# Linear attention, RMS norm and a SiLU feed-forward layer on one core: wider moves of w_out in every second tile, and shifted places for seven of its blocks

## The chip, the core and the metric

The kernel runs on one core of a Trainium2 chip. Its time is what the device takes for one execution, in microseconds (us); a time is the median of several runs. The profile is of one execution of its own. Its span goes from the first to the last instruction that it recorded.

## What is computed

Cut to what matters, the reference is this:

```python
# q, k, v: (8, 8, 576, 64) float32; w_in: (512, 2048), w_out: (2048, 512) float32
kv  = np.einsum('bhsd,bhse->bhde', k, v)
out = np.einsum('bhsd,bhde->bhse', q, kv)
rms = np.sqrt(np.mean(out * out, axis=-1, keepdims=True) + 1e-06)
x   = (out / rms * g_norm).transpose(0, 2, 1, 3).reshape(4608, 512)
h   = x @ w_in
g   = h * (1.0 / (1.0 + np.exp(-h)))
y   = g @ w_out          # (4608, 512) float32
```

The two products with `w_in` and `w_out` over 4608 tokens are nearly all of the work. This change concerns the second one.

## The kernel before

**Tiles.** The 4608 tokens are nine tiles `t` = 0 to 8 of TN = 512 tokens. The 2048 hidden columns are 16 blocks `f` of 128. Each number of the large products is held as an upper and a lower part in the type float32r, and a product is three matmuls: upper by lower, lower by upper, upper by upper.

**The first product.** In tiles 0 and 1 `products` makes a block of h from four pieces of x, twelve matmul pairs of 128x256 a block. From tile 2 on `pair_step` works on two blocks at a time (`i + 8` and `i`), with seven smaller products in the place of eight (lines 636 and 648): 42 matmuls of 128x256 in a step, eight steps in a tile.

**The second product.** `gate`, or `upper_part` and `lower_part`, make the activated block as `gh` (upper) and `gl` (lower), 128 x 512 each, in three buffers of the pool `gp`. `project` (line 521) multiplies it by one block `wo{f}` of `w_out`: for each of four groups `n` of 128 tokens it loads 128 columns of `gh` or `gl` into TensorE (the stationary operand; PEld in the profile), and moves 512 columns of `wo{f}` through it, into one PSUM bank `acc` of 512 columns. This is done for (gh, lower part of wo), (gh, upper part) and (gl, upper part). Each of the three goes through `halves` (line 483), which cuts the 512 columns into two matmuls of 256; each of the two comes with a load of the same stationary columns. So a block and a group take six matmuls of 128x256. In the last tile the fourth group has two banks of 256 columns, `acc` and `at`.

**The order.** The instructions run in the order in which the code is written. From tile 2 on a step's 42 matmuls are followed by `project` of the two blocks made one step before (`due`), eight groups of six matmuls, with the attention's own matmuls (lines 266 and 301 to 303) between them.

**Places in SBUF.** Where a tile begins in each partition follows from the order and the sizes of the pools. `gap` (line 80) is a tile that nothing uses; it moves those after it. A block of `wo` or `wi` has 2 x 512 x 4 = 4096 bytes, which is 16 x 256, so that in the kernel before all of `wo0` to `wo15` begin at the same place modulo 256, at 192. `x`, `x_second` and `operand`, which are moved in the first product, begin at 192 too; `wi`, `gh` and `gl`, whose columns are the stationary operand, begin at 0. The pieces begin at whole multiples of 512 bytes behind that.

**The scale.** `rsqrt` (line 442) works out the inverse root of the attention's sums by Newton steps on DVE. From batch 2 on it has two tiles of scratch of 72 columns, `m` and `u`.

Of the kernel before, what the change touches and what calls it, by code (L numbers as in the profile page):

```python
# [8 lines left out]
F32 = mybir.dt.float32  # L9
# [21 lines left out]
def linear_attention_rms_silu_ffn(  # L31
# [23 lines left out]
    B, NP, P, S = q.shape  # L55
    D = P // 2
    DM = NP * P
    NF = w_in.shape[0]
# [7 lines left out]
    weights = ctx.enter_context(tc.tile_pool(name="weights", bufs=1))  # L66
# [3 lines left out]
    small = ctx.enter_context(tc.tile_pool(name="small", bufs=2))  # L70
    gp = ctx.enter_context(tc.tile_pool(name="gp", bufs=LAG + 1))
# [5 lines left out]

    def gap(pool, size, name):  # L80
        pool.tile([P, size // 4], F32, name=name, bufs=1)

    def weights_places():
        for kind in ("wo", "wi"):
            for f in range(NF):
                block(kind, f, F32)
            if kind == "wo":
                gap(weights, 64, "gap_weights")

    gap(const, 128, "gap_first")  # L90
    gap(kvq, 192, "gap_q")
    gap(gp, 64, "gap_gated")
    kvm = [const.tile([P, P], F32, name=f"kvm{i}") for i in range(NP)]
    for t in kvm:
        nc.gpsimd.memset(t, 0.0)
# [4 lines left out]
    for i in range(4):  # L100
        nc.gpsimd.tensor_copy(
            out=both[32 * i:32 * i + 32, 32 * (i ^ 1):32 * (i ^ 1) + 32], in_=ident[32 * i:32 * i + 32, 32 * i:32 * i + 32]
# [36 lines left out]
    def block(kind, f, dtype):  # L139
        return weights.tile([P, 2, NP * P], dtype, name=f"{kind}{f}", tag=f"{kind}{f}")  # L140

    weights_places()

    def load_block(kind, f):
# [89 lines left out]
    def newton(y, u, m, eps=0.0):  # L234

        return [
            lambda: nc.vector.scalar_tensor_tensor(out=u, in0=m, scalar=eps, in1=y, op0=ALU.add, op1=ALU.mult),
            lambda: nc.vector.scalar_tensor_tensor(out=u, in0=u, scalar=-0.5, in1=y, op0=ALU.mult, op1=ALU.mult),
            lambda: nc.vector.scalar_tensor_tensor(out=y, in0=u, scalar=1.5, in1=y, op0=ALU.add, op1=ALU.mult),
        ]  # L240
# [201 lines left out]
    def rsqrt(sums, y, on_tensor):  # L442

        n = NP * (S // 32)
        sums, y = (t.rearrange("p c j -> p (c j)") for t in (sums, y))
        if on_tensor:
            bank = at_bank()
            m, u = bank[:, 0:n], bank[:, n:2 * n]
            nc.tensor.matmul(out=m, lhsT=both, rhs=sums, start=True, stop=True)
            calls = [lambda: nc.vector.tensor_scalar(  # L450
                out=m, in0=m, scalar1=float(D) * EPS, scalar2=None, op0=ALU.add
            )]
        else:
            m, u = (small.tile([P, n], F32, name=name, bufs=1) for name in ("m", "u"))
            calls = [
                lambda i=i: nc.vector.tensor_copy(
                    out=m[32 * i:32 * i + 32], in_=sums[32 * (i ^ 1):32 * (i ^ 1) + 32]
                )
                for i in range(4)
            ]  # L460
            calls.append(lambda: nc.vector.scalar_tensor_tensor(
                out=m, in0=m, scalar=float(D) * EPS, in1=sums, op0=ALU.add, op1=ALU.add
            ))
        calls.append(lambda: nc.vector.tensor_scalar(
            out=y.bitcast(I32), in0=m.bitcast(I32), scalar1=-0.5, scalar2=RSQRT_MAGIC, op0=ALU.mult, op1=ALU.add
        ))
        return calls + 3 * newton(y, u, m)
# [10 lines left out]
    def at_bank(tag=None):  # L478

        at_tags.append(at_tags.pop(0))  # L480
        return ps_at.tile([P, 512], F32, name="at", tag=tag or at_tags[-1])

    def halves(to, stationary, moving, start, stop):


        n = to.shape[-1]
        for at in range(0, n, 256):
            nc.tensor.matmul(  # L488
                out=to[:, at:at + 256], lhsT=stationary, rhs=moving[:, at:at + 256],
                start=start and at == 0, stop=stop and at == n - 256,  # L490
            )

    def products(hp, t, f, c):
        w = parts["wi", f]
        fs = slice(c * P, (c + 1) * P)
        for i, (a, b) in enumerate(((0, 1), (1, 0), (0, 0))):
            halves(
                hp[:, :TN], w[:, a, fs], x_part(t, b, c), c == 0 and i == 0, c == NP - 1 and i == 2
            )
# [12 lines left out]
    def sums_of(t):  # L512

        whole, half = slice(0, DM), (slice(0, DM // 2), slice(DM // 2, DM))
        banks = [(acc_bank(), n, whole) for n in range(TN // P)]
        if t == NT - 1:
            last, n, _ = banks.pop()
            banks += [(last, n, half[0]), (at_bank(), n, half[1])]
        return banks

    def project(t, f, gh, gl, bank, n, cs):
        first, last = order(t)[0], order(t)[-1]
        w = parts["wo", f]
        ns = slice(n * P, (n + 1) * P)
        bank = bank[:, :cs.stop - cs.start]
        for i, (g, a) in enumerate(((gh, 1), (gh, 0), (gl, 0))):
            halves(bank, g[:, ns], w[:, a, cs], f == first and i == 0, f == last and i == 2)
        if f == last:
            ob = tmp.tile([P, S], F32, name="ob", tag="tmp")[:, :cs.stop - cs.start]
            (nc.scalar.copy if n % 2 else nc.vector.tensor_copy)(out=ob, in_=bank)  # L530
            nc.sync.dma_start(out=out[t * TN + n * P:t * TN + (n + 1) * P, cs], in_=ob)
# [9 lines left out]
    def order(t):  # L541

        if t < 2:
            return [(f + t * HF) % NF for f in range(NF)]
        return [f for i in range(HF) for f in (i + HF, i)]
# [43 lines left out]
    def load_sums(i, *halves):  # L589

        for half in halves:
            to = place(f"sums{half}", half, F32R)
            nc.sync.dma_start(
                out=to.rearrange("p a j n -> p (a j n)").bitcast(F32),
                in_=sums_in_dram[i % HF, half].rearrange("p a n -> p (a n)"),
            )
# [72 lines left out]
    def pair_step(t, i, groups):  # L669
# [5 lines left out]
        def due(n):  # L675
            while n > 0 and groups:
                n -= (groups[0][-1].stop - groups[0][-1].start) / DM
                project(*groups.pop(0))
# [80 lines left out]
    def plan(b, g):  # L759
# [48 lines left out]
        if b == 1:  # L808
            at(chains, s, lambda: rsqrt(*norms, True))
        else:  # L810
            spread_out(lambda: rsqrt(*norms, False), 3 * s + 2, 6, 3, 3, 3)
# [11 lines left out]
    with tc.manual_schedule():  # L823

        first = [FirstPair(c) for c in range(NP)]
        stats = at_bank().rearrange("p (c i j) -> p c i j", i=2, j=8)
        second = plan(1, 3)
        for item in ORDER.split():
            kind, n = item.rstrip("0123456789"), int(item.lstrip("wiopbg") or 0)
# [150 lines left out]
        for t in range(NT):  # L980
            sums = sums_of(t)
# [6 lines left out]
            for step, f in enumerate(order(t)):  # L988
                g = t * NF + step
                for job in first_jobs.pop(g, ()):  # L990
                    job()
                for item in prepped:
                    split_block(*item, nc.scalar.copy)
                prepped = []
                if t == 0:
                    prepped = [("wi", f + 2)] * (3 <= f + 2 < NF) + [("wo", f)] * (f > 0)
                run(sum((bits(*item) for item in prepped), []), *[call() for call in chains.pop(g, ())])
                if t == 0 and 3 < f + 3 < NF:
                    magnitude("wi", f + 3)
                if t == 0 and f < WARM:  # L1000
                    hp = warm[f]
                    products(hp, t, f, NP - 1)
                else:
                    hp = h_bank()
                    for c in range(NP):
                        products(hp, t, f, c)
                pend.append(((t, f, *gate(t, hp)), sums))
                if t == 0 and f + 1 < NF:
                    magnitude("wo", f + 1)
                for job in mid_jobs.pop(g, ()):  # L1010
                    job()
                if len(pend) > LAG:
                    item, olds = pend.pop(0)
                    for old in olds:
                        project(*item, *old)
                for job in last_jobs.pop(g, ()):
                    job()
# [4 lines left out]
        for old in sums:  # L1022
            for item, _ in pend:
                project(*item, *old)
# [41 lines left out]
```

## Time and profile before

| | |
|---|---|
| median of 3 runs | 827.99 us (827.68 to 828.14) |
| the profiled execution | 827.72 us, its span 825.9 us |
| PE busy | 815.1 us (99%), 7518 instructions |
| PEld busy (loads of the stationary operand) | 808.5 us (98%), 7518 |
| DVE busy | 527.6 us (64%), 1027 |
| ACT busy | 358.4 us (43%), 744 |
| POOL busy | 145.6 us (18%), 142 |
| DMA | 122.81 MB, 149 GB/s over the span |

PE is TensorE's matmuls and PEld its weight loads, which overlap them. A matmul's end is modelled in the profile and lies behind the start of the next one, so the busy time of one matmul (276 ns) is not what it costs: that is the distance from its start to the next one's. A timeline row holds the start of its first instruction, the time to the end of its last, and after "x" how many it merges; the start of the next row minus its own start is what these took.

### The profile page before, as it was taken

How to read it: one execution, taken by the hardware profiler on the slowest of the kernel's cores; microseconds unless marked ns; L12 is line 12 of the kernel's file. 1: busy time of each engine (PE TensorE's matmuls, PEld its weight loads, DVE VectorE, ACT ScalarE, POOL GpSimd, SP SyncE). 2: the span in 40 equal slices, each digit the busy share in tenths (PEclk: the TensorE clock that was granted, in tenths of full speed). 3: DMA queues.
4: the chain of work that ended last, by engine and by line, in shares of the span. 5: the costliest groups of instructions: out<-in, count | busy, mean ns of one | idle time of the engine just before them, and what ended most of it. 6: DMA issues, size and time to landing. Idle time of an engine off the chain costs nothing.

```text
span 825.9 us, 18181 instructions
## 1 busy us (share of the span) xinstructions
PE 815.1 (99%) x7518; PEld 808.5 (98%) x7518; DVE 527.6 (64%) x1027; ACT 358.4 (43%) x744; POOL 145.6 (18%) x142
## 2 busy tenths in 40 slices
PE   8989999999999999999999999999999999999998
PEld 7889999999999999999999999999999999999998
DVE  4886884888476567757676668656765764464332
ACT  4766554534363255325442455225533423243222
POOL 2786883423020002000200011001100000000000
PEclk9999999999999999999999999999999999999999
DMA  8879011246352635364424453454423343334331
GB/s 324 321 245 380 7 42 70 102 182 233 126 177 95 218 120 169 103 214 149 168 77 163 161 182 103 143 177 160 143 92 104 108 159 106 106 106 155 103 103 52
DMA packets 42434, 122.81 MB, mean 149 GB/s; under 512 B 4848, under 2 KB 5104, under 8 KB 42352
## 3 DMA queue, kind: packets, MB, share of 16 engines
q1 hardware_dynamic: 42352, 121.65, 42.2%
q8 instruction: 59, 0.97, 0.5%
q14 instruction: 23, 0.19, 0.1%
HBM read 103.81 MB, written 17.83 MB: 147 GB/s over the span
## 4 chain that ended last, share of the span: by engine, by line
PE 94%; DMA 4%; POOL 1%; ACT 0%; issue 0%; SPq 0%
PE acc L488 46%; PE hp L654 32%; PE hp L488 9%; PE at L266 2%; DMA wo<-in_moe_w_out 1%; DMA k<-in_k 1%; DMA v<-in_v 1%; PE at L302 1%; PE at L303 1%; PE at L301 1%; DMA wi<-in_moe_w_in 1%; PE at L488 1%; DMA early_wi<-in_v 1%; PE at L299 1%; POOL wo L204 0%
## 5 line engine op out<-in xcount | busy, mean ns | idle before, releaser
L488 PE MATMUL acc<-wo,gh 128*128 128x256 f32 x2272 | 353.6, 277 | 0.0
L488 PEld LDWEIGHTS acc<-wo,gh 128*128 128x128 f32 x2272 | 302.1, 188 | 1.0 <-POOL wo L204 0.2
L488 PE MATMUL acc<-wo,gl 128*128 128x256 f32 x1136 | 222.9, 276 | 0.5 <-POOL gl L507 0.5
L488 PEld LDWEIGHTS acc<-wo,gl 128*128 128x128 f32 x1136 | 171.8, 188 | 0.7 <-POOL gl L507 0.7
L654 PE MATMUL hp<-x_second,wi 128*128 128x256 f32 x1344 | 163.1, 276 | 0.0
L654 PEld LDWEIGHTS hp<-x_second,wi 128*128 128x128 f32 x1344 | 157.2, 188 | 0.0
L654 PE MATMUL hp<-operand,wi 128*128 128x256 f32 x1008 | 123.3, 276 | 0.0
L654 PEld LDWEIGHTS hp<-operand,wi 128*128 128x128 f32 x1008 | 118.4, 188 | 0.0
L288 POOL TENSOR_TENSOR ql<-q,qh 128x576 fp32r<-128x576 f32 x24 | 35.3, 1472 | 368.2 <-ACT qh L287 321.7
L705 ACT COPY wi<-hp 128x256 f32<-128x256 f32 x56 | 20.8, 372 | 136.8 <-PE hp L654 136.8
L663 ACT ACTIVATE gh<-gf 128x512 fp32r<-128x512 f32 x56 | 35.4, 633 | 91.9 <-DVE gf L718 80.3
L663 ACT ACTIVATE gh<-wi 128x512 fp32r<-128x512 f32 x56 | 35.5, 634 | 76.6 <-DVE wi L718 66.3
L706 DVE TENSOR_TENSOR gf<-hp,wi 128x256 f32<-128x256 f32 x28 | 11.9, 425 | 81.6 <-ACT wi L705 81.6
L706 DVE TENSOR_TENSOR wi<-hp,wi 128x256 f32<-128x256 f32 x28 | 11.9, 425 | 81.2 <-ACT wi L705 81.2
L488 PE MATMUL hp<-x,wi 128*128 128x256 f32 x360 | 46.4, 283 | 1.4 <-POOL wi L204 1.4
L488 PE MATMUL hp<-x_second,wi 128*128 128x256 f32 x384 | 46.3, 276 | 0.0
L488 PEld LDWEIGHTS hp<-x,wi 128*128 128x128 f32 x360 | 43.5, 189 | 2.2 <-POOL wi L204 1.6
L667 DVE TENSOR_TENSOR gl<-wi,gh 128x512 fp32r<-128x512 f32 x56 | 38.4, 685 | 11.3 <-ACT wi L664 11.3
L488 PEld LDWEIGHTS hp<-x_second,wi 128*128 128x128 f32 x384 | 44.9, 188 | 0.1
L667 DVE TENSOR_TENSOR gl<-gf,gh 128x512 fp32r<-128x512 f32 x56 | 39.2, 700 | 7.4 <-ACT gf L664 7.4
L707 DVE TENSOR_TENSOR wi<-hp,wi 128x256 f32<-128x256 f32 x56 | 23.8, 425 | 29.5 <-PE hp L654 29.5
L307 ACT ACTIVATE sq<-at 128x256 f32<-128x256 f32 (+1 forms) x56 | 22.9, 410 | 44.5 <-PE at L303 35.7
(142 smaller groups left out, 1011.1 us busy)
## 6 DMA issues: line engine op xcount, KB each, us to landing
wi<-sums_in_dram SPq DMA_DIRECT2D x112, 512.0 KB, 3.3
out<-ob SPq DMA_DIRECT2D x35, 256.0 KB, 2.4
wi<-in_moe_w_in SPq DMA_DIRECT2D x16, 512.0 KB, 7.9
wo<-in_moe_w_out SPq DMA_DIRECT2D x16, 512.0 KB, 8.7
sums_in_dram<-sum_parts SPq DMA_DIRECT2D x16, 512.0 KB, 3.0
k<-in_k SPq DMA_DIRECT2D x28, 288.0 KB, 5.1
v<-in_v SPq DMA_DIRECT2D x28, 288.0 KB, 5.2
q<-in_q SPq DMA_DIRECT2D x28, 288.0 KB, 3.7
```

The source lines that it names most:

```text
L266: nc.tensor.matmul(out=self.kv[h], lhsT=self.k[rows, c, :], rhs=self.v[rows, c, :], start=(start and r == 0), stop=(stop and r == 4),)
L288: nc.gpsimd.tensor_tensor(out=self.ql, in0=self.q, in1=self.qh.bitcast(F32), op=ALU.subtract)
L299: nc.tensor.matmul(out=ps, lhsT=self.kvm, rhs=self.q[:, w], start=True, stop=True)
L301: nc.tensor.matmul(out=ps, lhsT=self.kh, rhs=self.ql[:, w], start=True, stop=False)
L307: nc.scalar.activation(out=self.sq[:, self.w], in_=self.ps, func=AF.Square)
L488: nc.tensor.matmul(out=to[:, at:at + 256], lhsT=stationary, rhs=moving[:, at:at + 256], start=start and at == 0, stop=stop and at == n - 256,)
L654: nc.tensor.matmul(out=out, lhsT=a_of(i, a, c), rhs=x[:, b, c], start=(n == 0), stop=(n == 5))
L663: nc.scalar.activation(out=gh, in_=x, func=AF.Silu)
L667: nc.vector.tensor_tensor(out=gl, in0=x, in1=gh.bitcast(F32), op=ALU.subtract)
L705: nc.scalar.copy(out=p1, in_=u)
L706: nc.vector.tensor_tensor(out=c1[:, low], in0=v, in1=p1, op=ALU.add)
L707: nc.vector.tensor_tensor(out=u2, in0=y, in1=p1, op=ALU.add)
```

## The change

In tiles 2, 4, 6 and 8 `project` has `halves` move 512 columns in one matmul; in tiles 0, 1, 3, 5 and 7 it moves 256 as before. The two banks of 256 columns of the last tile stay as they are. A gap of 32 bytes is put ahead of each of `wo9` to `wo15`, so that `wo9` begins at 224 modulo 256, and the next ones at 0, 32, 64, 96, 128 and 160; `wo0` to `wo8` stay at 192. The gap behind the `wo` blocks and that in `gp` grow, and `u` in `rsqrt` takes the place of the sums that it no longer needs (288 bytes less), so that every other tile stays where it was modulo 256.

```diff
     def weights_places():
         for kind in ("wo", "wi"):
             for f in range(NF):
+                if kind == "wo" and f > NF // 2:
+                    gap(weights, 32, f"gap{f}")
                 block(kind, f, F32)
             if kind == "wo":
-                gap(weights, 64, "gap_weights")
+                gap(weights, 96, "gap_weights")
...
-    gap(gp, 64, "gap_gated")
+    gap(gp, 96, "gap_gated")
...
-            m, u = (small.tile([P, n], F32, name=name, bufs=1) for name in ("m", "u"))
+            m, u = small.tile([P, n], F32, name="m", bufs=1), sums
...
-    def halves(to, stationary, moving, start, stop):
+    def halves(to, stationary, moving, start, stop, piece=256):
         n = to.shape[-1]
-        for at in range(0, n, 256):
+        piece = min(n, piece)
+        for at in range(0, n, piece):
             nc.tensor.matmul(
-                out=to[:, at:at + 256], lhsT=stationary, rhs=moving[:, at:at + 256],
-                start=start and at == 0, stop=stop and at == n - 256,
+                out=to[:, at:at + piece], lhsT=stationary, rhs=moving[:, at:at + piece],
+                start=start and at == 0, stop=stop and at == n - piece,
             )
...
-            halves(bank, g[:, ns], w[:, a, cs], f == first and i == 0, f == last and i == 2)
+            halves(
+                bank, g[:, ns], w[:, a, cs], f == first and i == 0, f == last and i == 2,
+                DM if t and t % 2 == 0 else DM // 2,
+            )
```

Two places show it in the order of TensorE's instructions; lines 488 and 492 are the matmul in `halves`, 301 to 303 (304 to 306 after) the attention's product for a later batch. The number behind a tile's name tells buffers apart, and "x4" is four equal instructions in a row. The first place is the first step of tile 2, before:

```order
L654 MATMUL hp_3255<-x_second_115,wi11_2919 128x256 x6
L301 MATMUL at_3323<-ql_3167,kh_3192 128x320
L302 MATMUL at_3323<-qh_3166,kl_3193 128x320
L303 MATMUL at_3323<-qh_3166,kh_3192 128x320
L488 MATMUL acc_3105<-wo8_1227,gh_3198 128x256 x4
L488 MATMUL acc_3105<-wo8_1227,gl_3200 128x256 x2
L488 MATMUL acc_3106<-wo8_1227,gh_3198 128x256 x4
L488 MATMUL acc_3106<-wo8_1227,gl_3200 128x256 x2
```

The same place on TensorE in the changed kernel:

```order
L661 MATMUL hp_3261<-x_second_115,wi11_2925 128x256 x6
L304 MATMUL at_3329<-ql_3173,kh_3198 128x320
L305 MATMUL at_3329<-qh_3172,kl_3199 128x320
L306 MATMUL at_3329<-qh_3172,kh_3198 128x320
L492 MATMUL acc_3111<-wo8_1234,gh_3204 128x512 x2
L492 MATMUL acc_3111<-wo8_1234,gl_3206 128x512
L492 MATMUL acc_3112<-wo8_1234,gh_3204 128x512 x2
L492 MATMUL acc_3112<-wo8_1234,gl_3206 128x512
```

Six matmuls of 256 columns have become three of 512; nothing has changed its place. This happens to 240 such groups of six. The second place is the end of tile 8 on TensorE in the changed kernel, where the third group is moved at 512 columns and the fourth, with its two banks, still at 256:

```order
L492 MATMUL acc_9104<-wo7_1149,gh_9841 128x512 x2
L492 MATMUL acc_9104<-wo7_1149,gl_9843 128x512
L492 MATMUL acc_9105<-wo15_1831,gh_9840 128x256 x2
L492 MATMUL acc_9105<-wo15_1831,gl_9842 128x256
L492 MATMUL acc_9105<-wo7_1149,gh_9841 128x256 x2
L492 MATMUL acc_9105<-wo7_1149,gl_9843 128x256
L492 MATMUL at_9106<-wo15_1831,gh_9840 128x256 x2
```

Here, too, only the width has moved. On ACT, POOL and the DMA queue the order and the shapes are the same in both kernels; on DVE 54 instructions of the Newton steps write or read `sums` where they had `u`.

## The prediction

> **What bounds the kernel now.** I read the page's busy times and clock first, then who waited for whom on TensorE, then the timeline of its matmuls.
>
> ```profile
> span 825.9 us, 18181 instructions
> PE 815.1 (99%) x7518; PEld 808.5 (98%) x7518; DVE 527.6 (64%) x1027; ACT 358.4 (43%) x744; POOL 145.6 (18%) x142
> PEclk9999999999999999999999999999999999999999
> PE 94%; DMA 4%; POOL 1%; ACT 0%; issue 0%; SPq 0%
> ```
>
> TensorE is busy for 99% of the span at the full granted clock, and it is 94% of the chain that ended last. The waits of PE (total, times, longest) are these, first and last row of seven:
>
> ```profile
> PE hp L844 <- POOL ident masks.py:199: 1.9, 1, 1.9
> ...
> PE acc L488 <- POOL gl L507: 0.5, 1, 0.5
> ```
>
> All seven together are 7.6 us. In the middle of the span there is no idle time at all (busy time of PE, PEld, DVE, ACT, POOL, then clock and DMA share):
>
> ```profile
> 300.00:400.00 100.00, 100.00 (x956) 99.60 (x951) 65.00 (x135) 43.43 (x97) 7.44 (x5) 1.00 0.45 150
> ```
>
> So the time is the sum over TensorE's matmuls of the distance from one start to the next, and the change is worth what it does to these distances. The timeline of a step in tile 3 gives the usual one:
>
> ```profile
> 270.36 0.62 PE L488 MATMUL acc<-wo,gh 128*128 128x256 f32 x4
> ...
> 273.08 2.20 PE L654 MATMUL hp<-operand,wi 128*128 128x256 f32 x18
> 275.12 2.09 PE L654 MATMUL hp<-x_second,wi 128*128 128x256 f32 x17
> ```
>
> From 270.36 to 273.08 lie four groups of six, 24 matmuls in 2.72 us, **113.3 ns** each; then 18 in 2.04 us, again 113.3. It isn't the only value that matmuls of this shape and these places take. In tile 0, with no clock loss and no transfer under way (the second fence, a row by stretches):
>
> ```profile
> 86.30 0.64 PE L488 MATMUL acc<-wo,gh 128*128 128x256 f32 x4
> ...
> 89.13 1.10 PE L488 MATMUL hp<-x,wi 128*128 128x256 f32 x8
> ```
>
> ```profile
> 86.30:89.10 2.80, 2.80 (x26) 2.80 (x25) 2.59 (x5) 2.60 (x6) 1.93 (x3) 1.00 0.00 0
> ```
>
> 24 matmuls take 2.83 us, **117.9 ns** each. PE is fully busy there and waits for nobody: the matmul and the load of the next stationary columns, which run beside each other, fit together less well. So 4.5 ns of a matmul hang on how these two reads meet, and the change alters that in two ways.
>
> **The change part by part.** What it touches is here:
>
> ```profile
> L488 PE MATMUL acc<-wo,gh 128*128 128x256 f32 x2272 | 353.6, 277 | 0.0
> L488 PE MATMUL acc<-wo,gl 128*128 128x256 f32 x1136 | 222.9, 276 | 0.5 <-POOL gl L507 0.5
> ```
>
> The two rows hold 3408 matmuls, and the last tile's bank `at` has 48 more: 3456 = 9 tiles x 16 blocks x 4 groups x 6.
>
> *The width.* Tiles 2, 4 and 6 have 64 groups of a block each, tile 8 has 48 of full width: 240 groups, and 720 pairs of matmuls that become one each. A pair now costs 2 x 113.3 = 226.7 ns. The trace has no float32r matmul of 512 columns. The nearest row is that of 320 columns, with the same 128x128 load beside it:
>
> ```profile
> 584.61 0.30 PE L301 MATMUL at<-ql,kh 128*128 128x320 f32 x1
> 584.75 0.31 PE L302 MATMUL at<-qh,kl 128*128 128x320 f32 x1
> 584.89 0.31 PE L303 MATMUL at<-qh,kh 128*128 128x320 f32 x1
> 585.04 0.63 PE L488 MATMUL acc<-wo,gh 128*128 128x256 f32 x4
> 585.50 0.39 PE L488 MATMUL acc<-wo,gl 128*128 128x256 f32 x2
> 585.73 0.62 PE L488 MATMUL acc<-wo,gh 128*128 128x256 f32 x4
> ```
>
> From 584.61 to 585.73 are three of 320 columns and six of 256: 1.12 us less 0.68 leaves 0.44, 147 ns each. That is 0.458 ns a column against 0.443 at 256: the longer move is no cheaper by the column, although it has fewer loads. At that rate 512 columns take 235 ns, 8 more than the pair: 720 x 8 = +5.8 us. The other end is a matmul that lasts about as long as one of 512 columns would and has one load of 128 columns under it, the plain float32 one of 256 columns (each is two records, which pass at a lower rate):
>
> ```profile
> 57.08 0.59 PE L299 MATMUL at<-q,kvm 128*128 128x256 f32 x2
> 57.32 0.82 PE L488 MATMUL acc<-wo,gh 128*128 128x256 f32 x4
> 57.98 0.40 PE L488 MATMUL acc<-wo,gl 128*128 128x256 f32 x2
> ```
>
> The 0.90 us hold two such passes and four of 256 columns at 113 to 118 ns (0.45 to 0.47): 215 to 225 ns a pass. At 215 a pair would save 11.7 ns, 720 x 11.7 = -8.4 us. A saving of 6.7 ns, if only the second half of the pair's two extra costs went, would be -4.8 us. I take the middle of 215 and 235, 225 ns: 720 x -1.7 = **-1.2 us**, ends -8.4 and +5.8.
>
> By the Trainium skill ("TensorE: Matmul & The Clock Gate", section "Back-to-back issue gap") a warm matmul of N columns takes N / 2.4 + 2.5 ns: about 109 ns at 256 and 216 at 512. The trace differs at 256, with 113.3. By the page alone a pair would fall from 226.7 to 216, some 7.7 us in all.
>
> *The change of width.* After the three of 320 columns six matmuls of 256 take 0.69 us (585.04 to 585.73) in the place of 0.68: about 10 ns to fall back into step. The widths change in 32 steps (8 in each of four tiles): **+0.3 us**, ends 0 and 1.
>
> *The places.* Seven blocks of `wo` now begin elsewhere relative to the stationary columns: by 32 bytes in `wo9` and in `wo15` (the other way round the 256), up to 128 in `wo12`. Matmuls of 256 columns on them: 7 blocks x 24 in each of tiles 0, 1, 3, 5 and 7, that is 840, and 7 x 6 in the last tile's fourth group: 882. No float32r row of the trace has other places than these, so the price is bounded: nothing, if places don't matter; 4.5 ns, if they bring the state at 86.30; twice that, +7.9 us, if the worst place is as far again from the better state. A gain can't be excluded (a place better than today's), and I bound it by the mirror of the 4.5 ns, -4.0 us. I take 4.5 ns, the one other value that steady matmuls of this shape show: 882 x 4.5 = **+4.0 us**. What the places do to the 315 pairs of 512 columns on these blocks is within the ends of the width's term.
>
> *The rest.* The scratch `u` becomes `sums`: 54 DVE instructions of the same shapes, hidden by TensorE (DVE is busy 65 of 100 us); without this cover they would still take as long as before. The loads of `wo9` to `wo15` land at other places, and none of PE's seven waits names them. The fewer matmuls come sooner by 1% of a tile at the most, which ACT and DVE, at 43% and 65%, follow.
>
> The sum is -1.2 + 0.3 + 4.0 = +3.1 us. Against the profiled execution, 827.72 us, that is 830.8; the median of the runs shown is 0.27 above it, so **831.1 us**.
>
> By the Trainium skill ("SBUF — State Buffer", section "Who interferes with whom") TensorE's two read ports, for the moving operand and for the weights, are independent. Then the places would cost nothing and the sum would be -0.9 us. The two distances, 113.3 and 117.9, for one shape at the same clock don't prove the opposite, but ask for something else that sets them.
>
> **The rivals.**
>
> *The long move hides its load and the places are free.* A load lasts about one 256-column matmul, so behind the first half of 512 nothing runs beside the move. For it speaks the 215 ns of the plain float32 pass, and that matmuls on 64 columns show no effect of the places:
>
> ```profile
> L266 PE MATMUL hp<-early_wo,early_wi 128*64 128x64 f32 x32 | 1.4, 228 | 1.0 <-DMA early_wo<-in_v 1.0
> L266 PE MATMUL hp<-early_wi,early_wo 128*64 128x64 f32 x32 | 1.4, 228 | 0.0
> ```
>
> Their operands begin at 192 and 0 and the other way round, with the same duration. Against it speaks the row of 320 columns. It gives 827.99 - 4.8 to -8.4: 819.6 to 823.2 us with free places, up to 826.3 where these take back a part. The page's 216 ns falls into this case.
>
> *The two cancel, or neither does anything.* 512 columns cost the two of 256 and the places little, or -4 stands against +4: within 1.65 us, 826.3 to 829.6.
>
> *The step is lost and stays lost.* At 86.30 the slower state holds over whole blocks, through both products, though only one meeting of load and move can have begun it. If a change of width or of place throws TensorE into it, the first product's matmuls, which the diff doesn't touch, pay too: 42 in each of 32 steps, 1344 x 4.5 = 6.0 us in the even tiles alone, 837 us with the forecast's sum; in all of tiles 1 to 8 about 5,900 x 4.5 = 26 us, 854 us. Against it: at 585.50 the six matmuls are back at 0.23 us a pair right behind the change of width. It decides as soon as steps behind a 512-column group show 118 ns.
>
> **How the numbers follow.** Forecast (the places cost more than the width saves): 36%, 829.6 to 834. Long move pays: 29%. Cancel: 22%. Step lost: 13%, 834 and more. What this kernel's measurement can tell from no change is about 0.2%, 1.65 us. So faster 29%, same 22%, slower 49%. The range leaves out the lower part of the second case (about 12%) and the upper part of the last (about 8%): 822.8 to 838.
>
> **What would show it.** A group of a block in tile 2 on `wo0` to `wo8` should take three times 225 ns, 0.675 us against 0.68: 0.65 says that the load is hidden, 0.70 that the rate of the 320 columns holds. In tile 3 a group on `wo9` to `wo15` should take 0.707 us, on the others 0.68. The 18 matmuls of a first product behind 512-column groups should take 2.04 us; 2.12 would be the lost step. The forecast is wrong if places cost nothing (0.68 in tile 3), or if the 512 columns take 220 or less.

## The result and the profile after

The changed kernel takes **841.09 us** (median of 4 runs, 840.82 to 841.19) against 828.07 before: a ratio of 1.0157 (95% interval 1.014 to 1.0175), +13.0 us. The forecast was 831.1, with a range of 822.8 to 838: the sign was right, the size four times too small, and the time lies above the range.

These lines of the page after answer to those shown of before: span, busy time by engine, granted clock, and the second product's groups, now in two widths (busy us, mean ns).

```profile
span 839.0 us, 16741 instructions
PE 829.0 (99%) x6798; PEld 790.0 (94%) x6798; DVE 530.6 (63%) x1027; ACT 358.8 (43%) x744; POOL 144.9 (17%) x142
PEclk9999999999999999999999999999999999999999
...
L492 PE MATMUL acc<-wo,gh 128*128 128x256 f32 x1312 | 209.0, 280 | 0.0
...
L492 PE MATMUL acc<-wo,gh 128*128 128x512 f32 x480 | 150.6, 395 | 0.0
L492 PE MATMUL acc<-wo,gl 128*128 128x256 f32 x656 | 131.2, 279 | 0.5 <-POOL gl L511 0.5
...
L492 PE MATMUL acc<-wo,gl 128*128 128x512 f32 x240 | 94.7, 394 | 0.0
```

TensorE has 720 matmuls and 720 loads less, PEld is busy 18.5 us less (790.0 for 808.5), the clock is full, PE is busy for 99% of the span as before and waits for nobody new. All of the 13 us are in the distances between matmuls. For 256 columns I call a distance of 113.3 ns the better step and 117.8 ns the slower one. The timeline shows three kinds of place. Tile 2, the 512-column group on `wo7` (at 192), and the first product behind it:

```profile
317.17 0.62 PE L492 MATMUL acc<-wo,gh 128*128 128x512 f32 x2
...
319.96 2.28 PE L661 MATMUL hp<-operand,wi 128*128 128x256 f32 x18
322.08 0.87 PE L661 MATMUL hp<-x_second,wi 128*128 128x256 f32 x6
```

From 317.17 to 319.96 lie twelve wide matmuls, 2.79 us: **232.5 ns** each, where two of 256 took 226.7. And from 319.96 to 322.08 the first product, which the diff doesn't touch, takes 2.12 us for 18: **117.8** in the place of 113.3, the slower step, as in the prediction's row at 86.30. In tile 3, first product and then `wo12` (at 64), 256 columns:

```profile
367.24 2.88 PE L661 MATMUL hp<-x_second,wi 128*128 128x256 f32 x24
369.96 0.63 PE L492 MATMUL acc<-wo,gh 128*128 128x256 f32 x4
...
372.79 0.40 PE L492 MATMUL acc<-wo,gh 128*128 128x256 f32 x2
```

The first product is at 113.3 here (2.72 us for 24), the 24 on the shifted block take 2.83: 117.9.

I added up the distances from each matmul's start to the next one's over both traces, by kind, and took the difference:

| kind of matmul | before, us | after, us | difference |
|---|---|---|---|
| wide in the changed kernel (720 pairs) | 163.6 | 167.7 | **+4.1** |
| 256 columns on shifted blocks (882) | 100.8 | 104.7 | **+3.9** |
| first product (untouched) | 358.6 | 362.0 | **+3.4** |
| 256 columns on `wo0` to `wo8` (untouched) | 132.5 | 134.2 | **+1.7** |
| attention at lines 301 to 303 | 18.6 | 19.0 | +0.3 |
| all others | 46.5 | 46.3 | -0.2 |
| sum | | | +13.1 |

So 8 us lie in what the diff changes, and 5.4 in matmuls that it doesn't.

### The profile page after: what moved, and what is told of

It reads as the page before. It is cut to its first block, busy times and chain, and to the rows that moved or that the text cites. A ratio compares the mean times of both kernels' runs of the same rounds, so it can differ in the third digit from the quotient of the medians.

```text
span 839.0 us, 16741 instructions
## 1 busy us (share of the span) xinstructions
PE 829.0 (99%) x6798; PEld 790.0 (94%) x6798; DVE 530.6 (63%) x1027; ACT 358.8 (43%) x744; POOL 144.9 (17%) x142
## 4 chain that ended last, share of the span: by engine, by line
PE 96%; POOL 1%; ACT 1%; DMA 1%; issue 1%; SPq 0%; DVE 0%; POOLq 0%
PE acc L492 47%; PE hp L661 32%; PE hp L492 10%; PE at L269 2%; PE at L304 1%; PE at L305 1%; PE at L306 1%; DMA early_wo<-in_v 1%; PE at L492 1%; PE hp L851 1%; PE at L302 1%; PE hp L269 0%; PE acc L357 0%; POOL wo L207 0%; PE acc L370 0%
## 5 line engine op out<-in xcount | busy, mean ns | idle before, releaser
L492 PE MATMUL acc<-wo,gh 128*128 128x256 f32 (+1 forms) x1792 | 359.6, 311 | 0.0
L492 PEld LDWEIGHTS acc<-wo,gh 128*128 128x128 f32 x1792 | 265.4, 188 | 19.3 <-POOL wo L207 0.2
L492 PE MATMUL acc<-wo,gl 128*128 128x256 f32 (+1 forms) x896 | 225.8, 310 | 0.5 <-POOL gl L511 0.5
L661 PE MATMUL hp<-x_second,wi 128*128 128x256 f32 x1344 | 164.6, 277 | 0.0
L661 PEld LDWEIGHTS hp<-x_second,wi 128*128 128x128 f32 x1344 | 158.7, 188 | 0.0
L492 PEld LDWEIGHTS acc<-wo,gl 128*128 128x128 f32 x896 | 145.6, 188 | 11.5 <-POOL gl L511 0.7
L661 PEld LDWEIGHTS hp<-operand,wi 128*128 128x128 f32 x1008 | 121.4, 188 | 2.2
L291 POOL TENSOR_TENSOR ql<-q,qh 128x576 fp32r<-128x576 f32 x24 | 34.7, 1444 | 376.8 <-ACT qh L290 362.0
L492 PE MATMUL hp<-x_second,wi 128*128 128x256 f32 x384 | 47.1, 279 | 0.0
L492 PEld LDWEIGHTS hp<-x_second,wi 128*128 128x128 f32 x384 | 45.7, 188 | 0.1
```

What stands on the lines that cost most here:

```text
L291: nc.gpsimd.tensor_tensor(out=self.ql, in0=self.q, in1=self.qh.bitcast(F32), op=ALU.subtract)
L492: nc.tensor.matmul(out=to[:, at:at + piece], lhsT=stationary, rhs=moving[:, at:at + piece], start=start and at == 0, stop=stop and at == n ...
L661: nc.tensor.matmul(out=out, lhsT=a_of(i, a, c), rhs=x[:, b, c], start=(n == 0), stop=(n == 5))
```

## Experiments

Each is told against the kernel before, run on the same chip beside it. Two theories were open at first: that the width, or that the places, begin the slower step in the untouched matmuls.

### The width alone

The change without its gaps; `u` stays, and the gaps behind `wo` and in `gp` are as before:

```diff
-                if kind == "wo" and f > NF // 2:
-                    gap(weights, 32, f"gap{f}")
...
```

> Only the width: 512 columns in tiles 2, 4, 6 and 8, every block of wo at 192 as in the kernel before. Theory of the width: a 512-column matmul costs 233 ns on wo0 to wo8 in the changed kernel, 6.3 more than two of 256, and would do so on all blocks: 720 x 6.3 = +4.5 us; and if the width is also what throws the first product into the 118 ns step, another 3 to 5 us, +8 to +9.5 in all (836 to 837.5). Theory of the places: the 233 ns come from the shifted blocks ahead of them, and without these a 512-column matmul takes 220 to 226.7: 0 to -4.8 us (823 to 828), with the first product at 113.3 everywhere.

Measured: 832.73 us against 828.0, ratio 1.0059 (1.0044 to 1.0074), +4.7. Twelve wide matmuls of tile 6:

```profile
644.67 0.63 PE L489 MATMUL acc<-wo,gh 128*128 128x512 f32 x2
...
647.47 0.73 PE L658 MATMUL hp<-operand,wi 128*128 128x256 f32 x5
```

2.80 us, 233.3 ns each; by kind the wide ones are +4.4 us, the first product +0.2 and the narrow second one +0.2. The wide move has a price of its own, 6 to 7 ns over the pair that it replaces, and behind the wide blocks of tiles 2, 4 and 6 the first product is in the better step.

### The places alone

The change without its width:

```diff
-                DM if t and t % 2 == 0 else DM // 2,
+                DM // 2,
```

> Only the places: wo9 to wo15 shifted, 256 columns everywhere. Matmuls of 256 columns on the seven blocks are now 7 x 24 x 9 = 1512. If the changed kernel's 118.6 ns hold for them: 1512 x 5.3 = +8.0 us, 836 us. Theory of the places for the lost step: the first product also shows steps at 118 ns behind them, +10 to +13 us (838 to 841). Theory of the width for the lost step: the first product is at 113.3 everywhere and the time is 836 at most. If the places cost nothing by themselves: 828.

Measured: 838.83 us, ratio 1.0132 (1.0115 to 1.0149), +10.8. By kind: shifted blocks +6.9 us, first product +1.8, narrow ones on `wo0` to `wo8` +2.0. So the places alone begin the slower step. The two parts don't simply add up (+4.7 and +10.8 for +13.0): where the 720 pairs lie, the width alone costs 4.4 us, the places alone 4.0, and both together 4.1. In tile 7 (the blocks come in the order of the program, `wo14` begins at 738.94 and `wo6` at 741.78):

```profile
738.94 0.64 PE L492 MATMUL acc<-wo,gh 128*128 128x256 f32 x4
...
741.78 0.64 PE L492 MATMUL acc<-wo,gh 128*128 128x256 f32 x4
...
744.61 2.28 PE L661 MATMUL hp<-operand,wi 128*128 128x256 f32 x18
746.73 2.99 PE L661 MATMUL hp<-x_second,wi 128*128 128x256 f32 x24
749.56 0.64 PE L492 MATMUL acc<-wo,gh 128*128 128x256 f32 x4
```

`wo14` takes 118.3 ns, `wo6`, which has its old place, 117.9, and the first product behind it 117.8 (2.12 us for 18, 2.83 for 24). In this run's trace as a whole the mean distances at 224, 0, 32, 64, 96, 128 and 160 are 118.2, 119.2, 116.8, 117.8, 119.5, 118.6 and 117.7 ns (without breaks of over 200 ns): none of the seven places is as good as 192.

### All blocks at one other place

The kernel before with the gap ahead of the `wo` blocks in the place of behind them:

```diff
+            if kind == "wo":
+                gap(weights, 64, "gap_weights")
             for f in range(NF):
                 block(kind, f, F32)
-            if kind == "wo":
-                gap(weights, 64, "gap_weights")
```

> All 16 blocks of wo begin at 0 modulo 256 in the place of 192; 256 columns everywhere, all else where it was. If a block's place relative to the stationary columns sets the distance, each of the 3456 matmuls takes what wo10 took in the changed kernel, 119.5 ns: 3456 x 6.2 = +21 us, 849 us. If it is the change from one block's place to the next's that costs, and a place held by all is free: 828 to 830 us. If wo10's 119.5 were the lost step and not the place: 113 to 118 mixed, 828 to 844.

Measured: 849.11 us, ratio 1.0255 (1.024 to 1.0271), +21.1, of which the second product is 19.7 by kind. One block of tile 6, and the start of the first product behind it:

```profile
698.60 0.64 PE L488 MATMUL acc<-wo,gh 128*128 128x256 f32 x4
...
701.48 2.22 PE L654 MATMUL hp<-operand,wi 128*128 128x256 f32 x18
```

24 matmuls in 2.88 us, 120.0 ns. The place itself has the price, not the change from one place to the next.

### Which operand's place?

Three runs move one operand, the other, or all. In these, and in the runs with four blocks and with one block further down, `u` is `sums`, as in the change, and the gap in `gp` makes up for it. First both `wo` (to 0, by the edit above) and `gh`, `gl` (to 64):

```diff
-    gap(gp, 64, "gap_gated")
+    gap(gp, 160, "gap_gated")
```

> As the run with all blocks of wo at 0, and gh and gl moved from 0 to 64 with them, so that the distance between moved and stationary operand is what it was before (192 behind). Theory of the relative place: 113.3 ns, 828 us within 2. Theory of the moved operand's own place: as the run with wo alone at 0 (849 if that holds).

Measured: 843.78 us, ratio 1.0191 (1.0176 to 1.0206), +15.8: neither. The steady 120.0 of `wo` at 0 is gone, and the second product shows 113.3 and 117.8 almost alone, mostly the latter, and the first product, which wasn't touched, +3.6 us. In tile 7 the two products change the step from one to the other:

```profile
694.40 0.64 PE L488 MATMUL acc<-wo,gh 128*128 128x256 f32 x4
...
697.23 2.22 PE L654 MATMUL hp<-operand,wi 128*128 128x256 f32 x18
699.29 2.88 PE L654 MATMUL hp<-x_second,wi 128*128 128x256 f32 x24
702.01 0.63 PE L488 MATMUL acc<-wo,gh 128*128 128x256 f32 x4
```

24 of the second product take 2.83 us, 24 of the first 2.72. So the relative place of the two operands decides between which two steps a product moves. That the products now lie apart by 64 bytes and so put each other out of step is a guess at this point. If it is right, moving everything must cost nothing:

```diff
-    gap(const, 128, "gap_first")
+    gap(const, 192, "gap_first")
...
-    gap(gp, 64, "gap_gated")
+    gap(gp, 96, "gap_gated")
...
```

> The kernel before with every tile of SBUF behind the first gap moved by 64 bytes: wo, x, x_second and operand begin at 0, wi, gh and gl at 64. If only the distance between the moved and the stationary operand counts, and its being the same in both products keeps the better step: 828 us within 1.7, 113.3 ns. If the moved operand's own place counts (wo at 0 gave 849): 840 and more.

Measured: 827.93 us against 828.04, ratio 0.9997 (0.9988 to 1.0007): no change. With `wo` at 0, the place that cost 21 us above:

```profile
702.64 0.62 PE L488 MATMUL acc<-wo,gh 128*128 128x256 f32 x4
...
705.36 2.20 PE L654 MATMUL hp<-operand,wi 128*128 128x256 f32 x18
707.40 0.84 PE L654 MATMUL hp<-x_second,wi 128*128 128x256 f32 x6
```

24 in 2.72 us, 18 in 2.04: 113.3. `wo`, `gh` and `gl` lie here at the same places modulo 256 as in the run before; what differs is the first product's operands and the smaller tiles. So the places of one product do set the step of the other, though no run shows how. As `u` is `sums` here too, that part of the change costs nothing. And with the loads moved alone, `wo` staying at 192:

```diff
-    gap(gp, 64, "gap_gated")
+    gap(gp, 160, "gap_gated")
```

> Only the stationary operand of the second product moves: gh and gl begin at 64, wo stays at 192, so the moved one lies 128 ahead of it, as wo14 did. Theory of the distance between the two: the price of wo14, 118.6 ns and more with the lost step, 3456 x 5.3 = +18 us, 846 us. Theory that only the moved operand's place counts: 828 us.

Measured: 845.47 us, ratio 1.021 (1.0194 to 1.0225), +17.4. The moved operand is where it was in the kernel before, and its matmuls slow down all the same:

```profile
706.31 0.64 PE L488 MATMUL acc<-wo,gh 128*128 128x256 f32 x4
...
709.16 0.52 PE L654 MATMUL hp<-operand,wi 128*128 128x256 f32 x3
```

24 in 2.85 us, 118.8, the price of `wo14`, which has the same distance. Within a product, what counts is the place of the moved operand **relative to the columns that are loaded**.

### Where the slower step begins, and how long it holds

Only `wo10` to `wo13` shifted, and then only `wo14`:

```diff
             for f in range(NF):
+                if kind == "wo" and f in {10: 64, 11: 32, 12: 32, 13: 32, 14: 96}:
+                    gap(weights, {10: 64, 11: 32, 12: 32, 13: 32, 14: 96}[f], f"gap{f}")
                 block(kind, f, F32)
```

```diff
             for f in range(NF):
+                if kind == "wo" and f in {14: 192, 15: 64}:
+                    gap(weights, {14: 192, 15: 64}[f], f"gap{f}")
                 block(kind, f, F32)
```

> Of the seven shifted blocks only wo10 to wo13 (0, 32, 64, 96); wo9, wo14 and wo15 stay at 192; 256 columns everywhere. In the run with the places alone the matmuls behind these four come back to 113.3 within a few, and those behind wo14 don't. Theory that the lost step is begun by wo14 and wo15: only the blocks' own price is left, 216 x (5.9 + 3.5 + 4.5 + 6.2) = +4.3 us, and some 0.7 for falling back, 833 us; the first product at 113.3 outside tile 0. Theory that any shifted block begins it by chance: four sevenths of +10.8, 834 us, with steps of the first product at 118.

> Only wo14 is shifted, to 128; all else at 192, 256 columns everywhere. Its own price is 216 x 5.3 = +1.1 us. Theory that it begins the lost step, which then holds until something else disturbs it: more than that, from +3 us (a few steps in each tile) to +15 (most of each tile), 831 to 843, with the first product at 118 behind wo14. Theory that each block pays for itself alone: 829.2 us.

Measured: four blocks 834.05 us, ratio 1.0072 (1.0057 to 1.0087), +6.0; one block **834.21** us, ratio 1.0074 (1.0057 to 1.0091), +6.2. With four blocks the own price is 4.0 us, and the rest lies in the other matmuls: the slower step does begin once in the first product, behind `wo11` in tile 1 (at 162.21 us), and ends with the attention's break at 213 us; from tile 2 on it doesn't. So no block is safe, and my sorting of them was half wrong. With one block the own price is 1.1 us, and 5.2 lie elsewhere. Its timeline in tile 6, from the first product ahead of `wo14` (651.30) to the one two blocks on, and then the same in tile 7:

```profile
648.58 2.88 PE L656 MATMUL hp<-x_second,wi 128*128 128x256 f32 x24
651.30 0.64 PE L490 MATMUL acc<-wo,gh 128*128 128x256 f32 x4
...
659.10 2.99 PE L656 MATMUL hp<-x_second,wi 128*128 128x256 f32 x24
661.92 0.28 PE L490 MATMUL acc<-wo,gh 128*128 128x256 f32 x1
```

```profile
733.30 2.99 PE L656 MATMUL hp<-x_second,wi 128*128 128x256 f32 x24
736.12 0.64 PE L490 MATMUL acc<-wo,gh 128*128 128x256 f32 x4
...
743.76 2.88 PE L656 MATMUL hp<-x_second,wi 128*128 128x256 f32 x24
746.48 0.39 PE L490 MATMUL acc<-wo,gh 128*128 128x256 f32 x2
```

24 of the first product take 2.72 us ahead of `wo14`, 2.82 behind it, still 2.82 ahead of the next `wo14`, 85 us later, and 2.72 behind that. In between, from `wo6` on, every matmul of both products is at 117.8, although nothing about them differs. One block, 24 matmuls, put TensorE into the slower step, and the same block took it out again.

### More wide moves, and wide moves at another place

Both runs have this edit in the run with the width alone; the second also has `wo` at 0, by the edit above.

```diff
-                DM if t and t % 2 == 0 else DM // 2,
+                DM if t else DM // 2,
```

> 512 columns in all of tiles 1 to 8, every block at 192: 1488 pairs in the place of 720. If the wide matmul has a price of its own, it goes with the count: 4.7 x 1488 / 720 = +9.7 us, 837.7 us, the first product at 113.3 (ten ns more at each change of width). If the price were in the alternation of wide and narrow tiles: +4.7 or less.

> The same 1488 wide matmuls, with all 16 blocks of wo at 0. In the changed kernel the wide ones on wo10 (at 0) took 228 ns against 233 on the others. If that is the place's doing and not wo10's: 1488 x 1.3 = +2 us, and 480 narrow ones at 119.5, +3 us: 833 us, against 849 for the same places with 256 columns; the wide move is then the better one where the place is bad. If 233 holds at every place: 840 us and more.

Measured: at 192, 837.85 us, ratio 1.0118 (1.0102 to 1.0133), +9.9: the price goes with the count. At 0, 841.5, ratio 1.0162 (1.0148 to 1.0176), +13.5, 8 more than I expected. The wide matmul did what it should:

```profile
672.81 0.62 PE L489 MATMUL acc<-wo,gh 128*128 128x512 f32 x2
...
675.53 2.28 PE L658 MATMUL hp<-operand,wi 128*128 128x256 f32 x18
677.65 2.99 PE L658 MATMUL hp<-x_second,wi 128*128 128x256 f32 x24
680.47 0.62 PE L489 MATMUL acc<-wo,gh 128*128 128x512 f32 x2
```

Twelve in 2.72 us: 226.7 ns each, which is the pair at 192. At 0 the pair costs 240 (two of 120.0), so there the wide move is the cheaper one: this run is 7.6 us faster than the one with all blocks at 0 and 256 columns (841.5 against 849.11). But the first product is at 117.8 behind almost every one of these groups (2.12 us for 18, 2.82 for 24): +10.3 us by kind. So the wide move's price, too, hangs on the place: it is dearer than the pair at 192 and cheaper than the pair at 0, and nowhere in these runs does it steadily take less than 226.7.

### A version that is faster than both

In the kernel before, tile 0 runs at the slower step from 80 to 117 us. First attempt: wide matmuls in tile 0 alone, for the last of the four groups of each block, by this edit in the run with the width alone.

```diff
-                DM if t and t % 2 == 0 else DM // 2,
+                DM if t == 0 and n == 3 else DM // 2,
```

> A version meant to be faster: the kernel before, with 512 columns only in tile 0 and there only for the last of the four groups of a block, 48 wide matmuls. In the kernel before some 445 matmuls of tile 0 run at 118 ns, 2.0 us in all. If a wide group brings the narrow ones behind it back to 113.3, as behind each wide group of the run with the width alone: -2.0 + 48 x 6.5 ns = -1.7 us, 826.3 us. If what holds tile 0 at 118 is something else: 828.3.

Measured: 830.12 us, ratio 1.0026 (1.0017 to 1.0035): slower by 2.15 us. From 80 us on, eight of these groups of three wide matmuls have narrow ones right ahead of them and the first product right behind. Seven of the eight turn the step over, from either side; the one on `wo6` finds the slower step and leaves it. The first product behind `wo6`, `wo7`, `wo9`, `wo10`, `wo11`, `wo13`, `wo14` and `wo15`, 24 matmuls each:

```profile
83.25 2.99 PE L489 MATMUL hp<-x,wi 128*128 128x256 f32 x24
...
88.89 2.89 PE L489 MATMUL hp<-x,wi 128*128 128x256 f32 x24
...
100.04 2.99 PE L489 MATMUL hp<-x,wi 128*128 128x256 f32 x24
...
105.68 2.89 PE L489 MATMUL hp<-x,wi 128*128 128x256 f32 x24
...
111.14 2.99 PE L489 MATMUL hp<-x,wi 128*128 128x256 f32 x24
...
125.08 2.99 PE L489 MATMUL hp<-x_second,wi 128*128 128x256 f32 x24
...
130.72 2.89 PE L489 MATMUL hp<-x_second,wi 128*128 128x256 f32 x24
...
136.18 2.99 PE L489 MATMUL hp<-x_second,wi 128*128 128x256 f32 x24
```

2.99 us to the end of the last is the slower step, 2.89 the better one: it goes to and fro, and the last group, on `wo15`, leaves the slower one behind; it holds from 136 us to the break at 213. So the width can begin the slower step too. The run with the width alone shows it in tile 8: behind nine wide matmuls on `wo9` the six narrow ones take 0.70 us (766.99 to 767.69), behind nine more on `wo1` 0.68 (769.79 to 770.47). In its tiles 2, 4 and 6, with 24 wide ones to a visit of the second product, the better step comes out.

The first attempt points to a single group, where the step is the slower one and no other follows:

```diff
-                DM if t == 0 and n == 3 else DM // 2,
+                DM if (t, f, n) == (0, 7, 3) else DM // 2,
```

> The kernel before with a single wide group: wo7 in tile 0, fourth group, three matmuls of 512 columns. In the run with 48 wide ones such a group of three turned the step over each time, from 113.3 to 118 and back, and the one on wo7 turned it from 118 to 113.3 at 88 us. The kernel before is at 118 from 80 to 117 us. If a group of three turns the step, the matmuls from 89 us on, about 245 up to the break at 117 us, come back to 113.3: -1.1 us and no loss behind, 826.9. If it does nothing to them: 828.0. If it turns a good step over: 829 and more.

Measured: **826.88** us against 827.99, ratio 0.9985 (0.9976 to 0.9994), as expected to 0.1 us. The first fence is this kernel, the second the one before, at the same place:

```profile
88.70 0.63 PE L489 MATMUL acc<-wo,gh 128*128 128x512 f32 x2
...
89.41 2.90 PE L489 MATMUL hp<-x,wi 128*128 128x256 f32 x24
92.14 0.62 PE L489 MATMUL acc<-wo,gh 128*128 128x256 f32 x4
```

```profile
88.42 0.64 PE L488 MATMUL acc<-wo,gh 128*128 128x256 f32 x4
...
89.13 2.99 PE L488 MATMUL hp<-x,wi 128*128 128x256 f32 x24
91.95 0.63 PE L488 MATMUL acc<-wo,gh 128*128 128x256 f32 x4
```

24 in 2.73 us for 2.82. The three wide matmuls themselves take as long as the six that they replace, which are in the slower step (0.71 us each time); the 1.1 us are saved behind them.

## Why the prediction failed

- **What bounds the kernel** was right: all of the difference is in the distances between matmuls, and no engine or transfer became late.
- **The width** had the wrong sign: -1.2 us forecast, +4.1 measured in the changed kernel and +4.4 to +4.7 alone. I set 225 ns as the middle between the plain float32 pass (215) and the rate of the 320-column matmul (235). The row nearest in kind was the 320-column one, the same type with the same loads, and it gave 235 against a measured 233. The plain float32 pass moves at another rate and should have been an outer end, not half of the mean. The 216 ns that the prediction quotes for 512 columns from the Trainium skill ("TensorE: Matmul & The Clock Gate", section "Back-to-back issue gap") stand there for a single matmul by itself, not for a stream of loads and matmuls; the streams here show 226.7 to 233.
- **The change of width** (+0.3) was small, as said: alone, +0.4 in all the narrow matmuls.
- **The places** were right in size: +4.0 forecast, +3.9 measured. That the size fits is luck: 4.5 ns is the second step at the old place, and the seven new places have prices of their own, 116.8 to 119.5 ns in the run with the places alone, whose mean happens to lie near it. The row of 64 columns that was quoted for free places is of plain float32 matmuls, not float32r, and compares durations, whose ends are modelled. By the Trainium skill ("SBUF — State Buffer", section "Who interferes with whom") the two read ports are independent and this term would be nothing; the run with the loads moved alone, 113.3 to 118.8 ns, differs, and the measurement decides.
- **The step that is lost and stays lost** was a rival at 13%, which the sum put at nothing, and it is what happened beside the other two: 5.4 us in untouched matmuls, near the 6.0 worked out for the even tiles, though it lay elsewhere and reached into odd tiles, so that the nearness is luck. In the run with the places alone the first product keeps the better step all through tiles 2 to 5, and so it does in the run with the width alone; in the changed kernel it turns to the slower one in tiles 2 and 4, behind the wide visits with the shifted `wo12` and `wo15`. There it takes both parts of the change. The row quoted against it, the quick return behind the 320-column matmuls at 585.50, showed one disturbance that the step survives, and I took it for all.
- **The range** ended at 838 since I let the terms exclude each other. Width, places and step add up: +4.1, +3.9, +5.4.

## What stays open

That the distance between matmuls depends on the place of the moved operand relative to the loaded columns is shown by the three runs that moved one, the other and all. What the two meet in, how one product's places reach the other's step, why seven groups of three turned the step and an eighth didn't, and what holds TensorE in one of two steps at the same places, isn't shown by any run: the profile has the loads' starts 2 to 5 ns behind the matmuls' in both steps. Places other than multiples of 32 bytes weren't tried.

## What to carry to other kernels

On a kernel that TensorE bounds, read the distance between matmul starts by shape and by block, not the busy time or the number of loads: fewer and longer matmuls can cost more, or less, by where their operands lie. Where two such distances occur for the same shape, find out what separates them before changing sizes or places, and price a change by what it does to the matmuls behind it too. A tile that is moved in memory, if only by 32 bytes, is a change to the time.

## What was not expected of the hardware

- A float32r matmul of 128x256 has two steady distances at the same places, 113.3 and 117.8 ns, and keeps either for as long as 85 us, over hundreds of matmuls and two different products.
- Within a product the distance depends on where the moved operand begins relative to the loaded columns: 113.3 or 117.8 ns at 192 (modulo 256), 116.8 to 120 at the seven other places; moving all operands by 64 bytes together changes nothing (827.93 against 828.04 us).
- A matmul of 512 columns takes 233 ns at 192, where two of 256 take 226.7, and 226.7 at 0, where two take 240: halving the loads lost time at the one place and saved it at the other. Three of them in a row turned the step of those behind over in seven of eight cases, in both directions.
